# New written order for the first two batches, idle products with a bank of their own, first k and scores in halves

## The chip, the core and the metric

The kernel runs on one core of a Trainium2 chip. The metric is the device time of one execution in microseconds (us), from all inputs in device memory to all outputs in device memory. The engines are named as the profile names them: PE multiplies matrices (PEld is its loading of weights), DVE, ACT and POOL work elementwise, SP issues the DMA transfers.

## The reference

Two layers of attention over 32 packed rows per head, then a max-of-three feed-forward layer, all in float32. Batch 8, 8 heads, 576 rows, head size 64; the scale is 1/8.

```python
def sm_attn(qq, kk, vv):
    s = scale * np.matmul(qq, kk.transpose(0, 1, 3, 2))
    s = s - np.max(s, axis=-1, keepdims=True)
    a = np.exp(s)
    a = a / (np.sum(a, axis=-1, keepdims=True) + 1e-09)
    return np.matmul(a, vv)
p_packed = sm_attn(p, k, v)
out = sm_attn(q, p_packed, p_packed)
...
x = out.transpose(0, 2, 1, 3).reshape(B * S, H * D)
h = np.maximum(np.maximum(x @ w1, x @ w2), x @ w3)      # 512 -> 768
return (h @ w_out).astype(np.float32)                   # 768 -> 512
```

## The kernel before

The work goes batch by batch. Each step has a letter and indices, the first index being the batch b in most of them:

- `S` (scores): p times k for all heads, into two tiles `s1_b_r`, one for each r (even and odd heads, which lie on partitions 0 to 63 and 64 to 127 of k). `A` (weigh, for b < 2 with `turn`): maximum on DVE, exponential on ACT, and in the first two batches a transpose on PE into the bank `tp` and a copy to `a1t`. From batch 2 on `X` does that transpose with DVE and 16 small DMAs (`spread`, tile `xt`). `Z` inverts the sums.
- `V` (values): a1t times v; `K` transposes the packed rows `pp` on PE into `pt_sb`; `Q` (queries): pt times q, in two halves `hf` of 288 columns.
- `C` j c converts one third of the weights of block j: the weights arrive as 64-bit words (load `w` j c, tile `wi`), and ACT (two instructions, L188 and L193), DVE (a shift, L202) and POOL (an add, L206) turn them into `w_sb`. `P` b j (project): pt times w_sb gives the layer-one weights folded with the packed rows, split into `ph` and `pl`.
- `B` b r hf (attend): the softmax of the second attention over 32 packed rows. DVE transposes, takes the maximum, subtracts, ACT exponentiates, DVE sums, inverts, multiplies and transposes back (`et`), and the result is split into `a2h` and `a2l`. Each letter in the text stands for one step of such a generator.
- `N` b j (layer_in): 36 products of 288 columns for each block j of hidden units, six for each of six tiles `mi`. `E` takes the maximum of three, `H` prepares operands, `W` prepares the output weights (loads `w6c`, array `wo`), `O` is the output layer (126 products), `F` sums and stores.

The order of all this is written out by hand as text. `START` holds the words for batches 0 and 1 and the first steps of batch 2, `LOOP` is run for each batch from 2 on. `run` goes through the words; every word issues the next step of its generator, so that the text sets the order of instructions on every engine's queue (loads are words too: they set the order on SP's queue). A suffix v, g or a puts an elementwise instruction on DVE, POOL or ACT instead of its default. Each engine works through its queue in order; it waits where an operand, a buffer or a PSUM bank is not there yet.

SBUF tiles come from pools with few buffers: six for incoming weights (`xs`), eight for k, v, q, a1t and others (`b`). PSUM has two double banks (`ps_big`) and four single ones (`ps_moe`), from which the `mi`, `mo`, first `tp` and first `pw` tiles are taken.

A word `I` n sets n idle products: 128-column products of the identity with itself, which nobody reads. The next step that calls `rouse` issues them into the bank that it is about to use, directly ahead of its own products:

Of the kernel before, what the change touches and what calls it, by code (L numbers as in the profile page):

```python
# [10 lines left out]
F32 = mybir.dt.float32  # L11
# [25 lines left out]
NX, NB, NY = 6, 8, 21  # L37
# [8 lines left out]


START = """
k00 k01 w02 I10 S0 A00 A00 k10 w00 C00 k11 Z00 w22 A00 w01 A01 A01 v01 Z01 C00 C02 C00 C01 v00 I4 S1 A10 A10
q000 C00 A11 I7 A01 A01v V01 C02 C02 A00v Z10 C01 C01 V01 q010 V00 C02 V00 K0 A11 Z11 C01 C22 C22 C22 K0 I1 Q0  # L50
B000 C22 B000 B000 B000 B010 B010 B000 q011 q001 I8 Q0 B011 B010 B010 w12 B001 B000v B000 B000g C12 I3 P00 P00
k20 B001 k21 B011 v11 B001 w10 B011 B010 B010 B000 B000g P00 P00 B001 B011 C12 C12 S2 B001 B000 B001 v10 B001
w11 B010 A21 B001g q10 q11 A21 I10 N00 A20 A20 B011 B010g B010 C12 B011 B011 B011g A10 A11 A10 A11 w21 C11 C11
V101 B010v C10 C10 B011 P00 B001 B001v w20 V101 B010 N00 E000 K1 w32 C11 K1v C10 N00 Q1 B001v C11 B10 C21 B11
C21 E000 E000 C20 N00 C10 P01 P01 B011g C21 C20 w42 C20 C32 w52 P01 B011 P10 X2 N00 N00 E001 E001 C32 C32 C42
C42 C42 C52 C21 w31 N01 E010v C20 w30 C31 C31 E001 B11 N01 v20 E010 N01 P02 C32 E010 C42 C31 C31 N01 w41 N01
w40 P02 P02 C30 E011 E011 C52 C52 N01 C30 P10 C30 X2 C41 C41 N02 P10 E011 N02 E020 E020 C30 B10 N02 C40 C41
Z21 E020 P03 P03 N02 E021 N02 w50 C50 C52 P03 N02 N03 N03 B10 w51 E021 E021 H01 N03 C50 C50 C40 C40 H00v B10
C41 B10 B10 B10 B11v N03 E031v C51 C51 C40 P04 E030v C51 C51 P11 P04 w64 B11 X2 E030 N03 N03 P04 N04 E031 E040
B11 B11 H02v N04 H02 C50 P05 v21 B10g E040 B11 B10 E031 C64 P05 B11g N04 N04 B11 B11 w61 N04 E041v C64 B10g  # L60
P05 B10 N04 C64 B11 w65 C61 w63 V201 E041 C65 C65 E040 E041 H04 H04 N10 E100v C65 N10 C61 C61 E100 Z20 V201
E030 N10 N10 N10 N10 C65 E101v P11 P11 N11 C64 q20 E101 q21 E101 w60 C60 C61 C60 E100 H04v E110v C60 C60 N11
N11 E110 E110 H10 N11 E111 W2v K2 w62 N11 E111 H10g K2 W0v W0 Q2 B20 B21 N11 N05 C63 H01v H00 C62 C62 C62 P13
E050 C63 W0v E111 B20 P12 P12 N05 C62 N05 N05 W0 E050 W2v E050 P12 W0v W2 N05 N05 N12 E051 H00 C63 C63 P13 W1
E120 N12 N12 E051 E051 N12 N12 W0 P14 B21 W2 P13 E120 E120 H03 P15 W2v W2g N12 E121 E121 W0v H01 W1 W1 W1 H02
N13 E121 N13 E130v E130 N13 N13 P14 N13 W1v W1 O0 P14 F0 E130 B20 O0 E131v N13 E131 H03v N14 N14 W1v H03v E131
W1v P15 B21 N14 E140v E140 W1g W1 W2v B21 B21 E140 F0 N14 O0 E141v P15 F0 O0 N14 N14 H05 H05v B20 H05v E141
H03 F0 H01 N15 O0 H12 N15 B20 H05 H13 E150v H01 W0 W2 O0 E141 F0 k30 F0 H03 H01v H14 H05 N15 N15 E151 E150
H03v N15 H05v E150 N15 O0 O0 H12 W0g E151 E151 H15 H13 H12v F0 O0 W2 H14 H13v W0v k31 F0 F0 O0 O0 O0 F0 F0 W2
O0 F0 F0 F0 H10v H14v H11 O0 O1 F1 O1 O1 F1 F1 B20v H15v F0 H15 B21 H11v H11v H13v H13 F0 H13v P20 H11 H11 P20  # L70
P20 H15 P22 P21 B21 P20 P20 O1 F1 H11v H15v O1 O1 H15v F1 F1 O1 B20 B20g O1 O1 F1 O1 F1 F1 B21g B21 B21 O1 F1
F1 O1 P22 P22 B21 P21 O1 F1 B20 P21 F1 B20 O1 F1 F1 B20v F1
"""


# [13 lines left out]
def fused_kernel(ctx: ExitStack, tc: tile.TileContext, kp, qt, va, vb, wi, wo, out):  # L89
# [46 lines left out]
    idle = [0]  # L136

    def rouse(ps):

        k = ps.shape[-1] // P  # L140
        for i in range(0, idle[0], k):
            n = min(idle[0] - i, k)
            nc.tensor.matmul(  # L143
                out=ps[:, 0:n * P], lhsT=ident, rhs=ident.unsqueeze(1).to_broadcast([P, n, P]),
                start=True, stop=True,
            )
# [6 lines left out]
        nc.sync.dma_start(out=t, in_=wi[j, c] if j < NJ else wo[c])  # L153
        staged[j, c] = t

    def load_k(b, g):
        u = b * G + g
        kt = pool.tile([P, 2 * S + 2 * 64], F32, name=f"kt{u}", tag="b", bufs=NB)
        nc.sync.dma_start(out=kt, in_=kp[u])
        loaded["k", b, g] = kt  # L160

    def load_v(b, g):
        u = b * G + g
# [76 lines left out]
    QUADS = [(g, pr) for g in range(G) for pr in range(2)]  # L240
    s1, a1, z1, a1t, av, pp, s2, a2 = {}, {}, {}, {}, {}, {}, {}, {}

    def scores(b):

        kt = [loaded.pop(("k", b, g)) for g in range(G)]
        s1[b] = [ps_big.tile([P, 2, 512], F32, name=f"s1_{b}_{r}", tag="big") for r in range(R)]
        rouse(s1[b][0][:, 0])
        for hf in range(2):
            for n, (g, pr) in enumerate(QUADS):
                for r in range(R):  # L250
                    o = slice(64 * r, 64 * r + 64)
                    w = 2 * S + 64 * pr + 32 * r
                    nc.tensor.matmul(  # L253
                        out=s1[b][r][32 * n:32 * n + 32, hf, 0:HS],
                        lhsT=kt[g][o, w:w + NP],
                        rhs=kt[g][o, pr * S + hf * HS:pr * S + (hf + 1) * HS],
                        start=True, stop=True,
                    )
        yield 0

    def weigh(b, r):

# [342 lines left out]
    def weigh_and_turn(b, r):  # L605
# [4 lines left out]

    stages = {
        "S": scores, "A": weigh_and_turn, "Z": invert, "X": spread, "V": lambda b, *rs: values(b, rs), "K": packed, "Q": queries,
        "B": attend, "C": convert, "P": project, "N": layer_in, "E": maximum, "H": halves,
        "O": layer_out, "F": finish, "W": weights,
    }
    loads = {"k": load_k, "v": load_v, "q": load_q, "w": load_w}
    begun = {}

    def run(words, base):

        for word in words.split():
# [66 lines left out]
```

## Time and profile before

| | us |
|---|---|
| median of 3 runs | 472.49 (471.71 to 473.06) |
| the profiled execution, its time | 472.98 |
| its span, first to last instruction | 471.2 |
| PE busy in it | 457.2 |
| DVE, POOL, ACT busy | 343.6, 218.6, 168.4 |
| scores of batch 3 (first instruction of the first LOOP) | at 147.75 |
| scores of batch 4 (first instruction of the second LOOP) | at 202.00 |

Lists of instructions are read as: start in us, duration in us, engine, line, operation, tiles written and read, shapes, how many were merged into one row, and in brackets how long the engine had been idle and what it waited for. A float32 product appears as two matmul records. Rows with a colon between two times are windows of the span: length, then for each engine its busy time and the number of instructions, then the granted clock of TensorE as a share of full speed (PEclk), the busy share of the DMA engines and GB/s. Rows of the chain that ended last have a start, a duration and the line. Groups have a count, the busy time in all and the mean in ns of one.

### The profile page before, as it was taken

How to read it: one execution, taken by the hardware profiler on the slowest of the kernel's cores; microseconds unless marked ns; L12 is line 12 of the kernel's file. 1: busy time of each engine (PE TensorE's matmuls, PEld its weight loads, DVE VectorE, ACT ScalarE, POOL GpSimd, SP SyncE). 2: the span in 40 equal slices, each digit the busy share in tenths (PEclk: the TensorE clock that was granted, in tenths of full speed). 3: DMA queues.
4: the chain of work that ended last, by engine and by line, in shares of the span. 5: the costliest groups of instructions: out<-in, count | busy, mean ns of one | idle time of the engine just before them, and what ended most of it. 6: DMA issues, size and time to landing. Idle time of an engine off the chain costs nothing.

```text
span 471.2 us, 11512 instructions
## 1 busy us (share of the span) xinstructions
PE 457.2 (97%) x4710; PEld 404.1 (86%) x4710; DVE 343.6 (73%) x722; ACT 168.4 (36%) x325; POOL 218.6 (46%) x193
## 2 busy tenths in 40 slices
PE   7799999999999999999999999999999999999996
PEld 2447887899989898989989898998989898998996
DVE  1669986987888678786777678776787667875652
ACT  3458855634233226122350225212260223402330
POOL 0467784776544055612564037421556036531642
PEclk9889999999999999999999999999999999999999
DMA  8998856002213640082303730064300820020002
GB/s 332 373 379 285 293 159 245 1 1 86 86 65 119 199 127 1 25 282 51 111 1 101 229 105 35 26 204 118 120 1 34 280 41 3 26 75 1 1 4 98
DMA packets 36580, 55.66 MB, mean 118 GB/s; under 512 B 17328, under 2 KB 27568, under 8 KB 36528
## 3 DMA queue, kind: packets, MB, share of 16 engines
q1 hardware_dynamic: 36528, 54.93, 35.4%
q8 instruction: 37, 0.61, 0.5%
q14 instruction: 15, 0.12, 0.1%
HBM read 41.94 MB, written 9.44 MB: 109 GB/s over the span
## 4 chain that ended last, share of the span: by engine, by line
PE 87%; DMA 6%; DVE 3%; ACT 1%; issue 1%; POOL 1%; SPq 1%; DVEq 0%; ACTq 0%; POOLq 0%
PE mi L475 45%; PE mo L544 29%; PE pw L439 7%; DMA wi<-in_wi 3%; DMA v<-in_va 2%; PE av L337 2%; DMA wi<-in_wo 2%; PE s L366 2%; PE s L253 1%; PE s L143 1%; DVE e L389 1%; DVE w_sb L202 1%; DVE r L489 0%; DVE xt L218 0%; PE tp L296 0%
## 5 line engine op out<-in xcount | busy, mean ns | idle before, releaser
L475 PE MATMUL mi<-a2h,ph 128*128 128x288 f32 x576 | 174.0, 302 | 0.6 <-ACT r L129 0.5
L475 PE MATMUL mi<-a2h,pl 128*128 128x288 f32 x576 | 170.0, 295 | 0.2 <-DVE pl L452 0.2
L475 PE MATMUL mi<-a2l,ph 128*128 128x288 f32 x576 | 169.8, 295 | 0.0
L475 PEld LDWEIGHTS mi<-a2h,ph 128*128 128x128 f32 x576 | 108.1, 188 | 15.6 <-issue 9.9
L475 PEld LDWEIGHTS mi<-a2h,pl 128*128 128x128 f32 x576 | 108.1, 188 | 0.7 <-DVE pl L452 0.7
L489 DVE TENSOR_TENSOR r<-mi,r 128x288 f32<-128x288 f32 x192 | 84.2, 449 | 33.3 <-PE mi L475 29.8
L475 PEld LDWEIGHTS mi<-a2l,ph 128*128 128x128 f32 x576 | 108.1, 188 | 0.0
L129 ACT COPY r<-mi 128x288 f32<-128x288 f32 x54 | 20.9, 398 | 120.3 <-PE mi L475 117.2
L452 DVE SCALAR_TENSOR_TENSOR pl<-pw,ph 128x768 fp32r<-128x768 f32 (+1 forms) x61 | 46.6, 772 | 3.2 <-ACT ph L450 2.6
L450 ACT ACTIVATE ph<-pw 128x768 fp32r<-128x768 f32 (+1 forms) x61 | 39.8, 674 | 15.2 <-PE pw L439 14.7
L513 POOL TENSOR_TENSOR r<-r 128x576 f32<-128x576 f32 (+1 forms) x29 | 35.2, 1225 | 20.5 <-issue 9.0
L544 PE MATMUL mo<-ych,xh 128*128 128x288 f32 x144 | 42.5, 295 | 0.0
L544 PE MATMUL mo<-ycl,xh 128*128 128x288 f32 x144 | 42.5, 295 | 0.0
L544 PE MATMUL mo<-ych,xl 128*128 128x288 f32 x144 | 42.4, 295 | 0.0
L134 POOL TENSOR_TENSOR yal<-r,yah 128x576 fp32r<-128x576 f32 x14 | 20.2, 1443 | 47.1 <-ACT yah L129 39.3
L439 PE MATMUL pw<-w_sb,pt 64*32 64x384 f32 x768 | 36.1, 487 | 0.8 <-POOL w_sb L206 0.4
L271 ACT ACTIVATE a<-s,nm 128x576 f32<-128x576 f32 x16 | 11.8, 740 | 65.9 <-DVE nm L267 65.9
L206 POOL TENSOR_TENSOR w_sb<-w_sb,wi 128x512 int32<-128x512 int32 x18 | 23.7, 1326 | 23.2 <-DVE w_sb L202 16.3
L131 DVE COPY r<-mi 128x288 f32<-128x288 f32 x42 | 18.9, 453 | 18.4 <-PE mi L475 18.3
L131 POOL CAST yah<-r 128x576 fp32r<-128x576 f32 x7 | 4.7, 674 | 56.4 <-DVE r L513 56.4
L544 PE MATMUL mo<-yah,xh 128*128 128x288 f32 x96 | 28.9, 301 | 0.0
L544 PE MATMUL mo<-ybl,xh 128*128 128x288 f32 x96 | 28.3, 295 | 0.0
(121 smaller groups left out, 871.6 us busy)
## 6 DMA issues: line engine op xcount, KB each, us to landing
kt<-in_kp SPq DMA_DIRECT2D x16, 640.0 KB, 4.0
wi<-in_wi SPq DMA_DIRECT2D x18, 512.0 KB, 7.6
v<-in_va SPq DMA_DIRECT2D x16, 512.0 KB, 5.7
q<-in_qt SPq DMA_DIRECT2D x14, 576.0 KB, 7.0
wi<-in_wo SPq DMA_DIRECT2D x6, 512.0 KB, 6.1
out_t<-r SPq DMA_DIRECT2D x8, 288.0 KB, 2.4
out_t<-t SPq DMA_DIRECT2D x8, 288.0 KB, 2.3
out_t<-s SPq DMA_DIRECT2D x8, 288.0 KB, 2.7
```

Source lines behind the costliest of these rows:

```text
L129: e.copy(out=out, in_=src)
L131: e.tensor_copy(out=out, in_=src)
L134: on(default).tensor_tensor(out=lo, in0=src, in1=hi.bitcast(F32), op=ALU.subtract)
L206: nc.gpsimd.tensor_tensor(out=dst.bitcast(I32), in0=dst.bitcast(I32), in1=up, op=ALU.add)
L271: nc.scalar.activation(out=a.rearrange("p (a b) -> p a b", a=2), in_=s[:, :, 0:HS], func=AF.Exp, bias=nm, scale=SCALE, accum_out=z,)
L439: nc.tensor.matmul(out=ps[r][NP * n:NP * n + NP, 0:NW * P], lhsT=pt_sb[b % 2][o, NP * n:NP * n + NP], rhs=w_sb[o, j, n * NW * P:(n + 1) * ...
L450: nc.scalar.activation(out=hi[:, r], in_=x, func=AF.Copy, scale=2.0 ** -WS)
L452: nc.vector.scalar_tensor_tensor(out=lo[:, r], in0=x, scalar=2.0 ** -WS, in1=hi[:, r].bitcast(F32), op0=ALU.mult, op1=ALU.subtract,)
L475: nc.tensor.matmul(out=sums[b, j, hf, x][:, 0:HS], lhsT=w[:, r, x * P:(x + 1) * P], rhs=a[:, c], start=(r == 0 and n == 0), stop=(r == R - ...
L489: nc.vector.tensor_tensor(out=h, in0=sums[b, j, hf, i][:, 0:HS], in1=h, op=ALU.max)
L513: less = lambda out, x, y: on("g").tensor_tensor(out=out, in0=x, in1=y, op=ALU.subtract)
L544: nc.tensor.matmul(out=ps[:, 0:HS], lhsT=w[:, x, m * P:(m + 1) * P], rhs=h[:, z], start=(p == 0 and i == 0), stop=(p == NQ - 1 and i == 2),)
```

## The change

Three things change.

1. `START` is written anew: nearly every word stands elsewhere. Batch 0 now goes first: k, q and v of batch 0 and the weights of blocks 0 and 1 are loaded ahead of k, v and q of batch 1. `LOOP` stays as it is, and `START` ends with the same steps done.
2. A new word `J` n issues n idle products at its own place in the order, into a single bank from `ps_moe` taken for them. `I` stays for the first ten.
3. k of batch 0 is loaded by halves of 64 partitions (`k` b g r), and `S0` has two steps, one for each r.

Numbers of lines: what stood at L253, L296, L337, L352, L366, L439 and L475 stands two lines further down in the changed file, the conversion (L188 to L206) one line.

```diff
 START = """
-k00 k01 w02 I10 S0 A00 A00 k10 w00 C00 k11 Z00 w22 A00 w01 A01 A01 v01 Z01 C00 C02 C00 C01 v00 I4 S1 A10 A10
-q000 C00 A11 I7 A01 A01v V01 C02 C02 A00v Z10 C01 C01 V01 q010 V00 C02 V00 K0 A11 Z11 C01 C22 C22 C22 K0 I1 Q0
...
+k000 k010 I10 S0 k011 A00 A00 J9 A00 q00 A00 w00 k001 J3 S0 A01 A01 v00 J9 A01 v01 Z01 C00 C00 Z00 w02 C02
+A01v V00 C00 V00 q01 V01 V01 J2 K0 C00 w01 w10 K0 C02 C02 J1 Q0 B010 C02 B010 B010v C01 C01 w11 B010 C10 C01
...
-    def load_k(b, g):
+    def load_k(b, g, r=None):
         u = b * G + g
-        kt = pool.tile([P, 2 * S + 2 * 64], F32, name=f"kt{u}", tag="b", bufs=NB)
-        nc.sync.dma_start(out=kt, in_=kp[u])
-        loaded["k", b, g] = kt
+        if ("k", b, g) not in loaded:
+            loaded["k", b, g] = pool.tile([P, 2 * S + 2 * 64], F32, name=f"kt{u}", tag="b", bufs=NB)
+        o = slice(0, P) if r is None else slice(64 * r, 64 * r + 64)
+        nc.sync.dma_start(out=loaded["k", b, g][o], in_=kp[u][o])
...
     def scores(b):
 
-        kt = [loaded.pop(("k", b, g)) for g in range(G)]
+        kt = [loaded["k", b, g] for g in range(G)]
         s1[b] = [ps_big.tile([P, 2, 512], F32, name=f"s1_{b}_{r}", tag="big") for r in range(R)]
         rouse(s1[b][0][:, 0])
-        for hf in range(2):
-            for n, (g, pr) in enumerate(QUADS):
-                for r in range(R):
...
-        yield 0
+        for rs in [(0,), (1,)] if b == 0 else [(0, 1)]:
+            for hf in range(2):
+                for n, (g, pr) in enumerate(QUADS):
+                    for r in rs:
...
+            yield 0
...
-        for word in words.split():
+        for at, word in enumerate(words.split()):
...
+            if kind == "J":
+                idle[0] = int(name[1:])
+                rouse(ps_moe.tile([P, 512], F32, name=f"idle{at}", tag="moe"))
+                continue
```

What the new text does to the queues is shown at three places. First, SP's queue at the start of the program (`kt0` and `kt1` are k of batch 0, `kt2` and `kt3` of batch 1, `v0`, `v1`, `q0`, `q1` batch 0, `wi0_2` the third third of the weights of block 0). Before:

```order
L159 DMA kt0_79<-in_kp 128x1280
L159 DMA kt1_81<-in_kp 128x1280
L153 DMA wi0_2_83<-in_wi 128x512
L159 DMA kt2_113<-in_kp 128x1280
L153 DMA wi0_0_115<-in_wi 128x512
L159 DMA kt3_118<-in_kp 128x1280
L153 DMA wi2_2_123<-in_wi 128x512
L153 DMA wi0_1_132<-in_wi 128x512
L165 DMA v1_141<-in_va 128x1024
L166 DMA v1_141<-in_vb 64x256
L165 DMA v0_151<-in_va 128x1024
```

The same place after the change:

```order
L161 DMA kt0_79<-in_kp 64x1280
L161 DMA kt1_81<-in_kp 64x1280 x2
L175 DMA q0_115<-in_qt 128x1152
L153 DMA wi0_0_120<-in_wi 128x512
L161 DMA kt0_79<-in_kp 64x1280
L166 DMA v0_140<-in_va 128x1024
L167 DMA v0_140<-in_vb 64x256
L166 DMA v1_154<-in_va 128x1024
L167 DMA v1_154<-in_vb 64x256
L153 DMA wi0_2_165<-in_wi 128x512
L175 DMA q1_194<-in_qt 128x1152
```

The v tiles of batch 0 moved ahead of most weights, and k of batch 1 to 17th and 19th place behind seven more weight loads.

Second, PE's queue between the packed rows of batch 0 (`av0` and `pa0_1`) and its first projection `pw0_0` (`s2_0_0` and `s2_0_1` are the two halves of the queries). Before:

```order
L352 MATMUL av0_199<-ident_67,pp0_230 128x128
L143 MATMUL s2_0_0_268<-ident_67 128x128
L366 MATMUL s2_0_0_268<-q0_180,pt0_73 32x288 x4
L366 MATMUL s2_0_0_268<-q1_232,pt0_73 32x288 x4
L143 MATMUL s2_0_1_293<-ident_67 128x512 x2
L366 MATMUL s2_0_1_293<-q0_180,pt0_73 32x288 x4
L366 MATMUL s2_0_1_293<-q1_232,pt0_73 32x288 x4
L143 MATMUL pw0_0_0_314<-ident_67 128x384
L439 MATMUL pw0_0_0_314<-w_sb_72,pt0_73 32x384
```

After:

```order
L354 MATMUL pa0_1_148<-ident_67,pp0_192 128x128
L143 MATMUL idle42_228<-ident_67 128x128
L368 MATMUL s2_0_0_230<-q0_115,pt0_73 32x288 x4
L368 MATMUL s2_0_0_230<-q1_194,pt0_73 32x288 x4
L368 MATMUL s2_0_1_253<-q0_115,pt0_73 32x288 x4
L368 MATMUL s2_0_1_253<-q1_194,pt0_73 32x288 x4
L143 MATMUL idle75_288<-ident_67 128x512 x2
L143 MATMUL idle75_288<-ident_67 128x384
L441 MATMUL pw0_0_0_292<-w_sb_72,pt0_73 32x384
```

The two halves of the queries now follow one another, and eleven idle products stand behind them (21 more stand between `pw0_0` and `pw0_1`, and `pw0_1` stands ahead of the first `mi`).

Third, SP's queue around the sixteen small transfers of `X2` (`xt2`), the output weights (`wi6_c`) and q of batch 2. Before:

```order
L153 DMA wi6_4_860<-in_wo 128x512
L319 DMA xt2_863<-x2_596 32x5x64 x8
L319 DMA xt2_863<-x2_596 32x4x64 x8
L165 DMA v5_929<-in_va 128x1024
L166 DMA v5_929<-in_vb 64x256
L153 DMA wi6_1_961<-in_wo 128x512
L153 DMA wi6_5_988<-in_wo 128x512
L153 DMA wi6_3_991<-in_wo 128x512
L174 DMA q4_1112<-in_qt 128x1152
L174 DMA q5_1115<-in_qt 128x1152
L153 DMA wi6_0_1118<-in_wo 128x512
L153 DMA wi6_2_1159<-in_wo 128x512
```

After:

```order
L166 DMA v4_926<-in_va 128x1024
L167 DMA v4_926<-in_vb 64x256
L153 DMA wi6_1_962<-in_wo 128x512
L153 DMA wi6_0_993<-in_wo 128x512
L321 DMA xt2_1022<-x2_823 32x5x64 x8
L321 DMA xt2_1022<-x2_823 32x4x64 x8
L153 DMA wi6_4_1108<-in_wo 128x512
L153 DMA wi6_5_1124<-in_wo 128x512
L175 DMA q5_1135<-in_qt 128x1152
L175 DMA q4_1163<-in_qt 128x1152
L153 DMA wi6_2_1190<-in_wo 128x512
L153 DMA wi6_3_1216<-in_wo 128x512
```

Two output-weight loads and v of batch 2 moved ahead of the sixteen transfers; two other output-weight loads stayed last.

More of the change, by code (lines that the diff above doesn't have):

```diff
@@ L48 @@
 START = """
-k00 k01 w02 I10 S0 A00 A00 k10 w00 C00 k11 Z00 w22 A00 w01 A01 A01 v01 Z01 C00 C02 C00 C01 v00 I4 S1 A10 A10
-q000 C00 A11 I7 A01 A01v V01 C02 C02 A00v Z10 C01 C01 V01 q010 V00 C02 V00 K0 A11 Z11 C01 C22 C22 C22 K0 I1 Q0
-B000 C22 B000 B000 B000 B010 B010 B000 q011 q001 I8 Q0 B011 B010 B010 w12 B001 B000v B000 B000g C12 I3 P00 P00
-k20 B001 k21 B011 v11 B001 w10 B011 B010 B010 B000 B000g P00 P00 B001 B011 C12 C12 S2 B001 B000 B001 v10 B001
-w11 B010 A21 B001g q10 q11 A21 I10 N00 A20 A20 B011 B010g B010 C12 B011 B011 B011g A10 A11 A10 A11 w21 C11 C11
@@ L54 @@
[L54 to L72, printed above, removed]
+k000 k010 I10 S0 k011 A00 A00 J9 A00 q00 A00 w00 k001 J3 S0 A01 A01 v00 J9 A01 v01 Z01 C00 C00 Z00 w02 C02
@@ new lines @@
+A01v V00 C00 V00 q01 V01 V01 J2 K0 C00 w01 w10 K0 C02 C02 J1 Q0 B010 C02 B010 B010v C01 C01 w11 B010 C10 C01
+C01 Q0 w12 C10 B001 B000 B001 B000 B001v B000v C10 C10 C11 C11 C11 B000 C11 B000 B010 w20 C12 J11 P00 P00 w22
+B011 P00 B000 B000 C12 B011 B001 P00 C12 C12 J21 P01 k10 B000 B000 B010 B001 C20 w32 k11 w21 B000 B000 B010
+B001 N00 B010 B010 B010g C22 C22 P01 P00 B010 N00 B001 B011v B001g v11 S1 v10 B011 P01 C32 C32 N01 N01 N01 C20
+B011 w30 E000v C22 B011v B001 E010 A11 A11 A10 A10 E010 Z11 B001v C21 C20 C21 C22 N00 B001v B011 E000 A10 A11
@@ new lines @@
+q10 A10v E000 q11 A11 N00 B011g B011 B011 V101 C20 C30 C30 w31 B011 Z10 E010 N01 V101 C21 C21 K1 C30 N00 w52
+C31 K1v C32 C32 Q1 N00 E011 E001 B10 C31 w41 P02 P02 B11 C52 P10 P10 B10 w40 B11 k20 C40 C41 C31 P02 N01 E011
+C30 N01 C31 P03 B10 P03 E001 E001 C41 N02 N02 E020 N02 C52 N02 E011 k21 N02 H00 w42 B10 B11 P10 E021 P03 S2
+C40 E020 C40 N03 N03 N03 v21 C41 C41 C42 E020 B11 C42 B10 E021 C52 E030 C42 A20 A20 A21 A21 w50 C50 w51 B11
+B11 B10 X2 X2 C50 C50 C51 N02 C52 N03 C40 C42 P04 C51 C50 B10 E030 E030 P11 B11 N03 B11g N03 C51 B10g P04 C51
@@ new lines @@
+P04 E031 N04 N04 N04 P05 E031 B11 v20 B11 E040v E040 B10 H01 H01v N04 N04 N04 E021 w61 C61 E031 P05 E041 P05
+N05 N05 N05 E040 w60 C60 B10g B10 B11 H00 N10 C61 E041 P11 Z20 E050 H00v X2 C60 C60 E041 C61 E050 P11 V201 Z21
+V201 N11 N11 K2 w64 N10 C61 E110v E110 E050 H01 H01 w65 C65 C65 N11 q21 N11 N10 K2 E100v N10 H04v H04 q20 Q2
+N11 w62 N10 E111 E110 C60 W0v N10 W0v W0v W0 w63 W0 H02v H02 E101 C65 P13 H04v B20 E100 B21 E101 C65 W0 E111
+E100 P12 N11 C62 C62 C63 C63 P13 C62 P12 W0v H03 C64 N05 C63 E101 N05 N05 C63 E051v P12 E051 C64 C64 P13 N12
@@ new lines @@
+N12 E111 C62 H01 H03v W1v W1v W1v N13 H02v N13 N13 E120 E130 P14 W1 P15 P15 E130 N12 C64 W2 W2 E051 N12 E121
+W1v N13 E131 E130 P14 W2v W2g W0 P15 E120 E120 N13 E131 W2v N12 E121 N12 E121 W0g W0 H05g P14 W2g O0 O0 W1 W2v
+B21 W2 N14 N14 W1v B20 N13 E131 H03 H05 F0 E140 O0 E140 F0 N14 E140 H12v H03v O0 k31 F0 N14 H05 N14 N15 N15
+N15 B20v H11 H05v E141 N14 E141 H01v W2 H10v W1v E150 B21v E150 E141 H03 F0 H03v W1g N15 N15 E151 E151 O0 H10g
+H10v H05 O0 H05v O0 B21 E150 W2 F0 F0 H13 H13 N15 E151 H14v O0 F0 F0 O0 B20 F0 O0 O0 B20 W1v H12 O0 F0 H12 H14
@@ L73 @@
+H11 F0 F0 F0 O0 H13v O0 H13v H13 H14 P20 P20 P22 F0 F0 H15 P21 H11v B21 F0 H15v P22 O1 O1 F1 k30 P20 O1 O1 O1
+O1 P21 H15v H15v H11v H15 H13v P22 H11g H11v B20v H15v O1 P20 F1 O1 B20 B20g O1 O1 O1 F1 O1 F1 B21 B21 F1 F1
+B21g F1 O1 F1 P20 B20 B20v O1 F1 F1 F1 B21 F1 F1 P21 F1 F1 B21 B21 B20v F1
 """
@@ L243, in scores @@
     def scores(b):
-        kt = [loaded.pop(("k", b, g)) for g in range(G)]
+        kt = [loaded["k", b, g] for g in range(G)]
         s1[b] = [ps_big.tile([P, 2, 512], F32, name=f"s1_{b}_{r}", tag="big") for r in range(R)]
         rouse(s1[b][0][:, 0])
-        for hf in range(2):
-            for n, (g, pr) in enumerate(QUADS):
-                for r in range(R):
[L251 to L258, printed above, removed]
-        yield 0
+        for rs in [(0,), (1,)] if b == 0 else [(0, 1)]:
+            for hf in range(2):
+                for n, (g, pr) in enumerate(QUADS):
+                    for r in rs:
+                        o = slice(64 * r, 64 * r + 64)
+                        w = 2 * S + 64 * pr + 32 * r
+                        nc.tensor.matmul(
+                            out=s1[b][r][32 * n:32 * n + 32, hf, 0:HS],
+                            lhsT=kt[g][o, w:w + NP],
+                            rhs=kt[g][o, pr * S + hf * HS:pr * S + (hf + 1) * HS],
+                            start=True, stop=True,
+                        )
+            yield 0
     def weigh(b, r):
```

## The prediction

> **What bounds the kernel now.** I read the page first, then windows of the span, then PE's list for the first 32 us, then the chain of waits.
>
> ```profile
> span 471.2 us, 11512 instructions
> PE   7799999999999999999999999999999999999996
> PEclk9889999999999999999999999999999999999999
> GB/s 332 373 379 285 293 159 245 1 1 86 86 65 119 199 127 1 25 282 51 111 1 101 229 105 35 26 204 118 120 1 34 280 41 3 26 75 1 1 4 98
> ```
>
> PE is full in 37 of 40 slices, so time can only come from the start, where it is not full or its clock is low, or from the last slice, which the change leaves alone.
>
> ```profile
> 7.50:9.50 2.00, 0.04 (x1) 0.04 (x1) 0.97 (x3) 0.83 (x2) 0.00 (x0) 1.00 1.01 417
> 14.50:19.60 5.10, 2.55 (x83) 1.79 (x85) 3.69 (x11) 4.37 (x9) 2.44 (x2) 0.97 1.06 323
> 19.60:26.10 6.50, 6.06 (x38) 2.15 (x42) 3.09 (x9) 1.66 (x4) 2.76 (x4) 0.50 1.04 409
> 31.40:61.30 29.90, 28.21 (x354) 22.02 (x352) 27.32 (x64) 24.37 (x48) 21.23 (x20) 1.00 0.81 285
> 61.30:100.90 39.60, 38.07 (x424) 33.24 (x417) 33.95 (x68) 21.46 (x37) 29.90 (x26) 1.00 0.35 117
> 100.90:147.80 46.90, 46.90 (x387) 44.80 (x393) 38.56 (x70) 17.14 (x31) 27.32 (x24) 1.00 0.19 60
> ```
>
> The columns are PE, PEld, DVE, ACT, POOL. From 19.6 to 26.1 the granted clock is 0.50. From 31.4 on PE loses 1.7 us, then 1.5, then nothing, and DVE is as good as full from 31.4 to 61.3. What PE does before that:
>
> ```profile
> 5.81 1.67 PE L253 MATMUL s<-kt 64*32 64x288 f32 x32
> 9.46 0.66 PE L296 MATMUL tp<-ident,a 128*128 128x128 f32 x4 [1.98 <-ACT a L271]
> 18.01 0.90 PE L337 MATMUL av<-v,a1t 128*32 128x64 f32 x40 [2.55 <-DMA v<-in_va]
> 18.84 1.09 PE L337 MATMUL pa<-v,a1t 128*32 128x64 f32 x40
> 20.37 0.48 PE L352 MATMUL av<-ident,pp 128*128 128x128 f32 x1 [0.44 <-DVE z L282]
> 21.20 1.21 PE L366 MATMUL s<-q,pt 64*32 64x288 f32 x16
> 22.34 3.78 PE L143 MATMUL s<-ident 128*128 128x512 f32 x4
> 26.05 0.72 PE L366 MATMUL s<-q,pt 64*32 64x288 f32 x16
> 29.32 2.42 PE L143 MATMUL mi<-ident 128*128 128x512 f32 x6
> 31.38 0.48 PE L475 MATMUL mi<-a2h,ph 128*128 128x288 f32 x1
> ```
>
> PE waits 2.55 us for v, the clock drops a microsecond later, and eight idle products at half clock (3.78 us) stand ahead of the second half of the queries, which starts at 26.05 instead of 22.4. The first useful large product starts at 31.38.
>
> ```profile
> 7.58 10.29 DMA v<-in_va
> 59.90 1.45 PE pw L439 x32
> 61.35 0.72 PE mi L475 x4
> 147.75 1.13 PE s L253 x32
> ```
>
> The chain runs through that v load. Two marks serve below. At 61.35 PE has just done the pair P04 and P11, with 132 products of `mi` behind it; in the new order the same pair stands behind exactly the same 132 products and the same other steps. At 147.75 the first LOOP starts, with equal work done in both orders; from there nothing changes.
>
> **The change, part by part.** The sum is made on the profiled execution (472.98, 0.49 above the median of the runs).
>
> *Loads.* By the GB/s row 3.9 MB have landed after one slice of 11.8 us, 8.3 after two, 12.8 after three. In the new order v of batch 0 is complete after 3.6 MB (about 11 us; before 17.87), all q of batch 0 after 4.7 (14 us), block 0 of the weights after 5.2 (15 us), block 1 after 6.8 (20 us), block 2 after 10.2 (29 us). The halved k adds two issues to SP's queue and the undivided q takes two away: nothing, since the ninth load waits for a free slot behind eight anyway.
>
> *Scores in halves.* Before, 16 products (32 records) of both r take 1.67 us; at full clock 1.13 (the row at 147.75). A half has 16 records. Lower bound 0.57 us; upper bound 1.13, since r = 0 and r = 1 lie on different halves of the partitions and would run side by side. I take 1.13. The Trainium skill, "TensorE: Matmul & The Clock Gate", Part 3 on packing small matmuls, speaks against the halves: products run concurrently when they lie in different row groups, and a half uses one group of 64 rows only. By that rule the two halves cost 2.26 together, by the record count 1.13; on the chain to the first product that is 1.1 us. No row of this trace has such a half.
>
> *Chain to the queries.* S0 for r = 0 ends at 5.8 + 1.1 = 6.9; maximum and exponential take until the transpose what they took before (7.48 to 9.46, 1.98), so the transpose is at 8.9. J9 fills that gap: idle products cost 2.02 us per ten at full clock (29.34 to 31.36), so J9 costs 1.8 and delays nothing. Transpose (0.8), J3 (0.6), second half of the scores (1.1) to 11.5; 1.98 more, covered by the second J9, to 13.5; transpose to 14.3, V00 and V01 with 0.9 each and the copy of a1t between them to 16.3. v is there since 11. From the end of V to the queries it took 19.93 to 21.20, 1.27: queries at 17.6. Since the gaps are filled, the clock should stay whole, and both halves (0.72 each) are done at 19.0, before at 26.8.
>
> *Queries to the first N.* DVE is the long pole. Its queue holds 21 instructions from the first transpose to `et`:
>
> ```profile
> L389 DVE STREAM_TRANSPOSE e<-s 128x288 f32<-128x288 f32 x32 | 13.9, 463 | 4.6 <-PE s L366 4.6
> L393 DVE TENSOR_REDUCE m<-e 128x9 f32<-128x288 f32 x4 | 1.7, 437 | 0.1
> L400 DVE TENSOR_REDUCE z<-e 128x9 f32<-128x288 f32 x4 | 1.8, 446 | 0.4 <-ACT e L397 0.4
> L395 DVE TENSOR_TENSOR e<-e,m 128x576 f32<-128x576 f32 x1 | 0.7, 694 | 0.0
> L452 DVE SCALAR_TENSOR_TENSOR pl<-pw,ph 128x384 fp32r<-128x384 f32 x26 | 13.7, 548 | 2.2 <-ACT ph L450 1.7
> L134 POOL TENSOR_TENSOR a2l<-et,a2h 128x288 fp32r<-128x288 f32 x3 | 2.4, 799 | 0.2
> L202 DVE TENSOR_SCALAR w_sb<-wi x18: 408/424/1442, 12.1 to 61.0; 128x512 uint32<-128x512 uint32 x18
> L206 POOL TENSOR_TENSOR w_sb<-w_sb,wi x18: 1281/1318/1397, 12.7 to 62.8; 128x512 int32<-128x512 int32 x18
> L188 ACT ACTIVATE wi<-wi x24: 647/678/717, 10.4 to 82.5; 128x512 f32<-128x512 f32 x24
> ```
>
> Five transposes (2.3), four maxima (1.75), three subtractions and one multiplication at half of 694 (1.4), four shifts (1.7), two sums (0.9), one `pl` (0.55), one reciprocal (0.2): 8.8 us from 18.3, so `et` at 27.1; the ACT cast (0.4) and `a2l` (0.8) follow to 28.3. The third weight piece of block 1 needs its DVE shift (about 26.1) and then 1.3 on POOL, so P01 ends near 27.8. J11 and J21 (32 idle products, 6.5 us) lie between 19.0 and 26.5 in that gap and are hidden; without that cover they would cost 6.5. First N at 28.0, before 31.38: −3.4. Ends: 26.5 if the halves take 0.57 and DVE's pairs overlap, 30.5 if ACT, which has ten conversion instructions of 0.68 in the same stretch, holds up the exponentials.
>
> *Work that changes sides.* Before, S1 and S2 (1.13 each) were done ahead of the first N, and P01 (0.72) behind it; now the other way round: +1.5 by the mark P04, P11. Between first N and that mark PE lost 3.5 us before (29.97 less 26.5 of work). In the new order I find: 0.9 at the transposes of batch 1 (DVE's maxima), 0.4 at V1, 0.5 at `a2l` of the first N, 0.9 at P03 and 1.1 at P04, whose last weight adds on POOL stand behind DVE shifts that follow B1's transposes and maxima. That is 3.8: no gain, no loss beyond 0.3. Mark at 61.35 − 3.4 + 1.5 + 0.3, about 59.7.
>
> *From the mark to the first LOOP.*
>
> ```profile
> 79.75 0.67 ACT L188 ACTIVATE wi<-wi 128x512 f32<-128x512 f32 x1 [4.74 <-DMA wi<-in_wo]
> 80.00:84.00 4.00, 2.96 (x46) 1.00 0.03 9
> 84.00:88.00 4.00, 3.60 (x48) 1.00 0.01 2
> 155.88 10.83 SPq L319 DMA_DIRECT2D xt<-x  x16
> ```
>
> ACT waits until 79.75 for an output-weight load, the copies of `mi` behind it come late, and PE loses 1.04 and 0.40 us. In the new order the two last loads still land near 80, but ACT's instructions for them stand behind the copies that PE needs until about 86. Between 0 and −1.4; I take −1.2, since they no longer meet. V2 waits for the sixteen transfers of X2: S2's end + 4.2 (maxima, exponentials, DVE transposes) + 10.83 + some 2 to land = 17; PE has 16.1 of work between S2 and V2, and the 1.1 of P04: no wait, without margin.
>
> *The rest.* Buffer and dictionary edits issue nothing. Idle banks are taken while only `tp` and `pw` use those four: nothing.
>
> Sum: −3.4 + 1.5 + 0.3 − 1.2 = −2.8; 472.98 − 2.8 = 470.2, on the median 472.49 − 2.8 = 469.7.
>
> **Rivals.**
>
> *A, the converter is the bound (no change).* DVE was busy 27.32 of 29.90 us from 31.4 to 61.3 and POOL adds cost 1.32 each. If P03 and P04 wait 2 us longer than I find, the start's gain is gone by the mark: 472.5. For it: block 3 and 4 are now due earlier, and DVE holds their shifts behind softmax work. Against it: POOL had 8.7 us free in that window.
>
> *B, V2 waits for the spread (slower).* In the new order S2 stands behind N02, where before it was done at 29. If the second DVE transpose of X2 ends 4.2 us later than S2's end + 4.2, the gain is gone and 1.4 more: 473.9 and up; every further microsecond goes straight into the time, since V2 stands in PE's queue. For it: there is no margin, and DVE's queue is full. Against it: only maxima, a sum and two shifts stand ahead there.
>
> *C, the clock drops anyway.* If the 0.50 comes from the small products of V and Q and not from the gap of 2.55 us, it also meets the new order: 6.5 us at half clock lose 3.3, which makes 473.0. Against it: small products at 5.8 to 15 ran at 1.00, also behind the gap of 1.98 us from 7.5 to 9.5. The Trainium skill, the same page, Part 1 on the clock gate, speaks of an idle window of about 3.4 us before the clock is halved. By that the gap of 2.55 in this trace would be too short to be the cause, which would favour C; the trace has the drop right behind the gap.
>
> *D, a larger gain.* PE's waits behind the first N shrink by 1.5 and the first N comes at 26.5: 466.7.
>
> **How the numbers follow.** About 0.3% (1.4 us) is what a measurement of this kernel can tell from no change. Forecast (1.4 to 4.4 us faster) 0.55; D 0.12; A 0.13; C 0.06; B 0.14. Faster 0.67, same 0.19 (A and C), slower 0.14. Predicted 469.7. The range leaves out the outer part of D and of B: 466.2 (D with the whole 1.4 of the late stall) to 474.0; the forecast alone is 468.1 to 471.1.
>
> **What would show it.** First `mi` product near 28.0 (no later than 29.5); PEclk 1.00 from 6 us on; queries at 17.6 with no idle products between the halves; P04, P11 pair ending near 59.7; no wait of PE for `wo` between 78 and 88; first LOOP's scores near 145. Wrong it would be by a clock of 0.50 after 16 us, by PE waiting more than 2 us at P03 or P04 for POOL, or by V2 waiting for `xt`.

## The result, and the profile after

The changed kernel takes 469.86 us (median of 9 runs, 468.8 to 471.68), the kernel before 472.6 beside it: a ratio of 0.9942 (95% interval 0.9919 to 0.9964). The forecast was 469.7. The total is right; several steps under it are not, and that their errors cancelled is luck. The experiments found a version at 466.7.

Each run reports its mean granted clock. In three of the nine runs it is 0.994 to 0.996 and the time 471.5 to 471.7; in six it is 0.998 to 1.000 and the time 468.8 to 470.2. The profiled execution (471.49, span 469.7) is one of the three. Three executions far above all others are left out of every comparison below (634 us at a clock of 0.657, which is the one with the trace of e1_whole_k, 883 us and 2516 us). The page of the profiled execution:

```profile
span 469.7 us, 11526 instructions
PEclk9899999999999999999999999999999999999999
GB/s 220 372 360 341 397 93 288 3 22 35 36 148 155 165 124 1 27 285 62 96 1 115 219 125 11 27 223 103 118 1 43 278 34 2 27 75 1 1 4 98
```

PEclk was 8 in the second and third slice before; the third is now whole, but the dip in the second is still there, where the forecast said there would be none. The first figure of GB/s is the other surprise: 220, before 332. Windows of 2 us (columns as before: PE, PEld, DVE, ACT, POOL, granted clock, DMA share, GB/s), first of the kernel before, then of the changed one:

```profile
4.00:6.00 2.00, 2.00 (x8) 0.83 (x10) 0.00 (x0) 0.00 (x0) 0.00 (x0) 1.00 1.01 411
6.00:8.00 2.00, 1.48 (x32) 0.44 (x24) 0.47 (x1) 0.00 (x0) 0.00 (x0) 1.00 1.02 422
```

```profile
4.00:6.00 2.00, 2.00 (x6) 0.75 (x6) 0.00 (x0) 0.00 (x0) 0.00 (x0) 1.00 1.00 210
6.00:8.00 2.00, 2.00 (x17) 0.79 (x18) 0.00 (x1) 0.00 (x0) 0.00 (x0) 1.00 0.94 258
14.00:16.00 2.00, 2.00 (x6) 0.84 (x3) 0.91 (x2) 0.50 (x1) 0.00 (x0) 0.50 1.05 327
```

The DMA engines are as busy in both (share about 1.0), yet move half as much from 4 to 6 us (210 against 411 GB/s), while the half loads of k are at the head of the queue. PE's list of the profiled execution, with the products of Q2 and of the first LOOP at its end:

```profile
13.06 1.32 PE L255 MATMUL s<-kt 64*32 64x288 f32 x16 [1.73 <-DMA kt<-in_kp]
14.31 3.71 PE L143 MATMUL idle<-ident 128*128 128x512 f32 x6
18.50 1.83 PE L339 MATMUL pa<-v,a1t 128*32 128x64 f32 x80
21.45 1.21 PE L368 MATMUL s<-q,pt 64*32 64x288 f32 x32
31.98 0.40 PE L477 MATMUL mi<-a2h,ph 128*128 128x288 f32 x1
59.60 1.52 PE L441 MATMUL pw<-w_sb,pt 64*32 64x384 f32 x32
80.58 1.21 PE L368 MATMUL s<-q,pt 64*32 64x288 f32 x32 [1.03 <-DMA q<-in_qt]
146.22 1.20 PE L255 MATMUL s<-kt 64*32 64x288 f32 x32
```

PE waits for the second half of k until 13.06. The clock then falls (0.50 from 14 to 16 us), and the second J9 takes 3.71 where 2.21 is its length at full clock. The first mi product comes at 31.98, later than before (31.38), and the time was won behind it.

The same kernel, profiled once more (e8_changed_again, 469.96, clock 0.999), shows the ordinary case without the dip; it is the one to hold against the forecast:

```profile
5.92 1.70 PE L255 MATMUL s<-kt 64*32 64x288 f32 x16
12.30 1.17 PE L255 MATMUL s<-kt 64*32 64x288 f32 x16 [1.28 <-DMA kt<-in_kp]
13.40 2.21 PE L143 MATMUL idle<-ident 128*128 128x512 f32 x6
16.18 1.84 PE L339 MATMUL pa<-v,a1t 128*32 128x64 f32 x80
19.14 1.20 PE L368 MATMUL s<-q,pt 64*32 64x288 f32 x32
29.76 0.40 PE L477 MATMUL mi<-a2h,ph 128*128 128x288 f32 x1
57.45 1.52 PE L441 MATMUL pw<-w_sb,pt 64*32 64x384 f32 x32
70.35 1.44 PE L339 MATMUL av<-v,xt 128*32 128x64 f32 x74 [0.33 <-DMA xt<-x]
78.97 1.29 PE L368 MATMUL s<-q,pt 64*32 64x288 f32 x32 [1.31 <-DMA q<-in_qt]
144.68 1.20 PE L255 MATMUL s<-kt 64*32 64x288 f32 x32
```

From the first LOOP to the end nothing changed: 471.2 − 147.68 = 323.5 before, 468.2 − 144.68 = 323.5 here.

### The profile page after: what moved, and what is told of

The parts are those of the page before. It is cut to its first block, busy times and chain, and to the rows that moved or that the text cites. A ratio compares the mean times of both kernels' runs of the same rounds, so it can differ in the third digit from the quotient of the medians.

```text
span 469.7 us, 11526 instructions
## 1 busy us (share of the span) xinstructions
PE 460.6 (98%) x4726; PEld 407.0 (87%) x4726; DVE 344.7 (73%) x727; ACT 168.7 (36%) x331; POOL 212.1 (45%) x182
## 4 chain that ended last, share of the span: by engine, by line
PE 83%; DMA 5%; DVE 5%; SPq 3%; issue 1%; POOL 1%; ACT 1%; POOLq 0%; DVEq 0%
PE mi L477 42%; PE mo L546 29%; PE pw L441 6%; SPq L321 2%; DMA kt<-in_kp 2%; PE av L339 2%; PE s L368 2%; DMA wi<-in_wi 2%; PE s L255 1%; DMA q<-in_qt 1%; PE idle L143 1%; POOL w_sb L207 1%; DVE w_sb L203 1%; DVE mx L268 1%; DVE pl L454 0%
## 5 line engine op out<-in xcount | busy, mean ns | idle before, releaser
L129 ACT COPY r<-mi 128x288 f32<-128x288 f32 x61 | 23.7, 400 | 122.4 <-PE mi L477 122.3
L515 POOL TENSOR_TENSOR r<-r 128x576 f32<-128x576 f32 (+1 forms) x23 | 26.9, 1180 | 17.3 <-issue 9.0
L131 DVE COPY r<-mi 128x288 f32<-128x288 f32 x35 | 15.9, 456 | 18.2 <-PE mi L477 18.1
L515 DVE TENSOR_TENSOR r<-r 128x288 f32<-128x288 f32 (+1 forms) x49 | 27.1, 556 | 2.3 <-POOL ybl L134 1.7
```

The lines of the kernel that those rows point to most:

```text
L129: e.copy(out=out, in_=src)
L131: e.tensor_copy(out=out, in_=src)
L515: less = lambda out, x, y: on("g").tensor_tensor(out=out, in0=x, in1=y, op=ALU.subtract)
```

## Experiments

The theory after the result (R): a load that touches only 64 partitions moves at half the rate, and holds up what is queued behind it. The rivals: the place of the last half behind q and w (P), the converter as the bound (C), and that all of the gain is the clock (K). The letter C stands for the converter in this section only; the prediction calls that rival A.

**k loaded whole, scores still in halves (e1_whole_k).**

```diff
-k000 k010 I10 S0 k011 A00 A00 J9 A00 q00 A00 w00 k001 J3 S0
+k00 k01 I10 S0 A00 A00 J9 A00 q00 A00 w00 J3 S0
```

> The changed kernel with both k of batch 0 loaded whole (128 partitions each) as the first two transfers, ahead of q and w; the first scores still in two halves. Theory R (rate): a load that touches only 64 partitions moves at about half the rate, 210 GB/s where the kernel before had 411 from 4 to 6 us, and holds up all loads queued behind it; that made the second half of k land at 13.0. By R the GB/s from 2 to 8 us go back to about 290, 410, 420; both k are there near 5.9; the second half of the scores starts at 10.5 to 11 with no wait of PE for k; no 0.50 of the clock; queries near 18.5; first mi product at 28 to 29.5 instead of 31.98; the pair P04, P11 ends 1.0 to 2.5 earlier than 61.05; time 0.9 to 2.5 us below the changed kernel, 467.4 to 469.0. Rival C (the converter is the bound): the start comes as early, but PE then waits the same 2 to 3 us more at P01 to P04 for weights, the pair ends at 61 and the time stays within 0.5 us of 469.9. Rival P (place in the queue): the half load was late only because q and w stood ahead of it; then the rate from 2 to 8 us is about as low as in the changed kernel, since what sets it would not be the halves.

Measured: 467.93, ratio to before 0.9901 (0.9877 to 0.9926), 1.9 us below the changed kernel, as R said; C, which allowed 0.5, is out. Only its time is used here, so what R said of its single steps is not shown by this run.

**The last half load moved to the front (e1b_half_k_early).**

```diff
-k000 k010 I10 S0 k011 A00 A00 J9 A00 q00 A00 w00 k001 J3 S0
+k000 k010 I10 S0 k011 k001 A00 A00 J9 A00 q00 A00 w00 J3 S0
```

> The changed kernel with its four half loads of k kept, but the last of them moved ahead of q and w. Theory R: four loads of 320 KB at about 210 GB/s take some 6.2 us, so the last half of k is there near 9; PE does not wait for it at 10.5 to 11; q, w and v stay as late as in the changed kernel (the sum of bytes and rates is the same), v complete near 15; low rate from 2 to 8 us and none of the dip to 208 from 10 to 12; first mi product 29 to 30.5; time between e1_whole_k and the changed kernel, 468 to 469.5. Rival P: the rate from 2 to 8 us is 290 to 420 now, because nothing but the place was wrong, and k is complete near 6. Rival C: time within 0.5 us of 469.9 here as well.

Measured: 469.62, ratio 0.9939 (0.9917 to 0.9962). Windows, then PE:

```profile
4.00:6.00 2.00, 2.00 (x6) 0.76 (x6) 0.00 (x0) 0.00 (x0) 0.00 (x0) 1.00 1.00 210
6.00:8.00 2.00, 2.00 (x18) 0.79 (x19) 0.44 (x1) 0.00 (x0) 0.00 (x0) 1.00 1.01 205
10.00:12.00 2.00, 2.00 (x22) 0.76 (x19) 0.00 (x0) 0.74 (x2) 0.00 (x0) 1.00 1.03 412
```

```profile
10.84 1.17 PE L255 MATMUL s<-kt 64*32 64x288 f32 x16
28.82 0.85 PE L441 MATMUL pw<-w_sb,pt 64*32 64x384 f32 x8 [0.39 <-POOL w_sb L207]
29.60 0.40 PE L477 MATMUL mi<-a2h,ph 128*128 128x288 f32 x1
```

PE's wait for k is gone, but the rate is low for as long as half loads run and then doubles: the halves set it, not the place, and P is out. The time I gave was 468 to 469.5, a hair too low, and rival C would have had it (within 0.5 of 469.9); it is e1_whole_k that speaks against C. The first mi product comes only 0.16 earlier than in e8_changed_again. What PE no longer waits for k, it loses at P01, which takes from 27.58 to 29.60 here and 1.0 there: it waits for the weight add on POOL, which ends at 28.76 here and at 28.93 there. ACT, which converts these weights first, waits for their loads 1.47, 0.84 and 1.08 long (14 to 22 us; 0.42 and 0.21 there). So half loads cost twice: by the wait for k, and by the weights that stand behind them in the queue.

**Part three undone (e2_whole_scores).** The line of START as in e1_whole_k without the second S0, and:

```diff
-        for rs in [(0,), (1,)] if b == 0 else [(0, 1)]:
+        for rs in [(0, 1)]:
```

> The third part of the change undone: k loaded whole and the first scores of both halves in one step, as before, all else of the new order kept. Theory R: as e1_whole_k; the scores take 1.67 at 5.8 in one piece, the second transpose can start a microsecond earlier, first mi product within 1 us of e1_whole_k; time within 0.8 us of e1_whole_k, so halving the scores buys nothing without the loads. Rival H: the halves of the scores are worth their order, and this run is over 1 us slower than e1_whole_k. Rival C: 469.4 to 470.4.

Measured: 466.78, ratio 0.9882 (0.9855 to 0.9908); 1.15 below e1_whole_k. That is more than the 0.8 I allowed, and rival H, which had it slower, is out.

```profile
4.00:6.00 2.00, 2.00 (x8) 0.75 (x10) 0.00 (x0) 0.00 (x0) 0.00 (x0) 1.00 1.03 416
5.92 1.66 PE L255 MATMUL s<-kt 64*32 64x288 f32 x32
13.39 1.83 PE L339 MATMUL pa<-v,a1t 128*32 128x64 f32 x80
26.91 0.40 PE L477 MATMUL mi<-a2h,ph 128*128 128x288 f32 x1
54.72 1.52 PE L441 MATMUL pw<-w_sb,pt 64*32 64x384 f32 x32
141.70 1.20 PE L255 MATMUL s<-kt 64*32 64x288 f32 x32
```

The scores of both halves take here (1.66) what the first half alone takes in e8_changed_again (1.70), so the half loads did not even bring the first half sooner. The second half costs 1.10 more (12.30 to 13.40): the halves of the scores cost 1.1, their loads the rest. The first mi product is 2.85 earlier, the pair P04, P11 2.73, the first LOOP 2.98: all of it reaches the end, and the converter keeps pace even then. (The two traces are of different chips; e9_whole_again, this kernel on the chip of e8_changed_again, has the first mi product at 26.68 and the first LOOP at 141.69.)

**Part three alone, in the old order (e4_before_halves).**

```diff
-k00 k01 w02 I10 S0 A00 A00
+k000 k010 k011 k001 w02 I10 S0 S0 A00 A00
```

> The kernel before with part three alone: the four half loads of k in place of two whole ones at the head of the queue, and the first scores as two steps one behind the other; the order of all else is that of before. Theory R: k is complete near 8.8 instead of 5.8, everything queued behind it lands some 3 us later (v of batch 0 near 20.5 instead of 17.87), PE's wait for v grows by as much, and the time is 2 to 4 us above before, 474.5 to 476.6. Rival P (the halves cost nothing by themselves): time within 0.5 us of 472.6, k there near 6. Rival: the clock falls one step earlier in the longer gap, then up to 5 us above.

Measured: 476.05, ratio 1.0059 (1.0029 to 1.009): slower, as R said.

```profile
6.00:8.00 2.00, 1.48 (x16) 0.57 (x16) 0.47 (x1) 0.00 (x0) 0.00 (x0) 1.00 1.01 203
9.39 2.11 PE L255 MATMUL s<-kt 64*32 64x288 f32 x16 [1.91 <-DMA kt<-in_kp]
20.82 0.90 PE L339 MATMUL av<-v,a1t 128*32 128x64 f32 x40 [1.80 <-ACT a L273]
```

The second half of the scores begins at 9.39, where before both halves began at 5.81 and were done at 7.48. The products of v come 2.8 later than at 18.01, behind ACT's exponential and not, as I expected, behind v. The wait of 1.91 was enough for the clock to fall to 0.50 (from 10 to 16 us).

**The idle steps taken out of e2_whole_scores (e3_no_idle_steps, e10_no_idle_again).** All J words are dropped from START.

> e2_whole_scores without its seven idle steps (J9, J3, J9, J2, J1, J11, J21), all else the same; PE then stands idle some 2 us before each of the first two transposes, 2.5 us before P00 and 4.5 us before P01. Theory K (the idle products are worth their clock): the granted clock falls to 0.50 in at least one of the longer gaps; if it falls before P01, P01 and the first 3 us of mi products run at half speed and the time is 1.5 to 3 us above e2_whole_scores, 468.3 to 469.8; in the runs where it falls the mean granted clock is 0.993 to 0.997. Rival N (they are worth nothing): clock 1.00 at the first mi product, which comes at 26.9 or earlier, and the time stays within 0.5 us of 466.8. Rival W (idle steps delay work): first mi product 0.3 to 1 us earlier than 26.91 and the time below 466.4.

Measured: 468.33, ratio 0.9910 (0.9889 to 0.9931), with a clock of 0.982 to 0.989, further down than the 0.993 to 0.997 I gave. It ran on another chip than e2_whole_scores, so both were run again side by side, with the changed kernel:

> e3_no_idle_steps again, on one chip with e9_whole_again, which alone it is compared with. Theory K: 1 to 2 us above e9_whole_again, since first mi product came at 28.61 and not 26.91 with the clock at 0.50 in three stretches. Rival N: within 0.5 us of it.

> e2_whole_scores again, beside the changed kernel and the kernel without idle steps on one chip. Theory R: 2 to 3.5 us below e8_changed_again, clock 0.998 to 1.000 in every run. In e5_late_q2 the pair P04, P11 and the product behind it waited 1.0 us in all (at 54.65 and 58.33) where e2_whole_scores did not; if that belongs to the chip, it shows here too and the time is 467.5 to 468; if it belongs to the moved Q2, the time is 466.5 to 467.

> The changed kernel itself, on one chip with the next three. In its profiled execution the clock fell to 0.50 from 14 to 17 us behind a wait of 1.73 us for the second half of k. Theory R: the wait is in every run, since the loads are the same; whether the clock falls varies from run to run: granted clock 0.998 to 1.000 where it does not and 469 to 470.3, 0.994 to 0.996 where it does and 471.3 to 471.8. Rival: the wait is an accident of that one run, then the first mi product is at 28 to 29 and the time 468.

Measured on one chip: before 472.99, without idle steps 468.42 (ratio 0.9925, 0.9897 to 0.9953), with them 466.71 (0.9883, 0.9858 to 0.9907), the changed kernel 469.81 (0.9943, 0.9923 to 0.9963). So the idle steps are worth 1.7 us, and the granted clock of each run says the same: 0.981 to 0.989 without them, 0.998 to 1.000 with them. The dip of the changed kernel, which I expected in some of its runs, was in none of these eleven (clock 0.998 to 1.000), though the wait for k was there in the one with a trace, 1.28 long. The trace without idle steps, and behind it the same place in e9_whole_again:

```profile
12.00:14.00 2.00, 2.00 (x48) 1.28 (x46) 1.48 (x6) 0.85 (x3) 0.14 (x1) 0.54 1.00 363
11.71 0.74 PE L298 MATMUL tp<-ident,a 128*128 128x128 f32 x4 [1.45 <-ACT a L273]
20.66 0.87 PE L441 MATMUL pw<-w_sb,pt 64*32 64x384 f32 x12 [2.30 <-POOL w_sb L207]
23.23 2.74 PE L441 MATMUL pw<-w_sb,pt 64*32 64x384 f32 x8 [1.71 <-POOL w_sb L207]
26.27 1.51 PE L441 MATMUL pw<-w_sb,pt 64*32 64x384 f32 x8 [0.30 <-POOL w_sb L207]
27.71 0.61 PE L477 MATMUL mi<-a2h,ph 128*128 128x288 f32 x1
```

```profile
25.77 0.98 PE L441 MATMUL pw<-w_sb,pt 64*32 64x384 f32 x16
26.68 0.40 PE L477 MATMUL mi<-a2h,ph 128*128 128x288 f32 x1
```

The idle products hold up no real work: in e9_whole_again P01 begins at 25.77, as they end, and the last weight add that it needs ends on POOL at 25.85. Without them PE waits for the weights of P00 and P01 in the same places, the clock falls to 0.50 from 24 to 28 us, and the first mi product comes 1.0 later.

**Only the gap filled, in the old order (e7_before_filled_gap, e11_before_short_fill).** J12, then J5, ahead of the first V01 of before, with the changed kernel's code for J:

```diff
-q000 C00 A11 I7 A01 A01v V01 C02
+q000 C00 A11 I7 A01 A01v J12 V01 C02
```

> The kernel before with one thing added: an idle step of 12 products (2.4 us) behind the second transpose, where PE waits 2.55 us for v; order, loads and scores as before. Theory K (what the changed kernel gained is the clock): the 0.50 from 19.6 to 26.1 is gone, the eight idle products between the halves of the queries take 1.6 instead of 3.78, the second half starts at 23 to 24 instead of 26.05, first mi product near 29, and the time is 470.0 to 471.0, so the changed kernel's gain of 2.7 would nearly all be had without the new order. Theory O (the order of loads and steps): the second half of the queries then waits for its q load or the first mi product for DVE and POOL; first mi product 30.5 or later, time 471.8 to 472.5, and the new order's gain is its own.

Measured: 472.11, ratio 0.9988 (0.9975 to 1.0001). The time is in the range of theory O, but not for its reason: the idle step was too long for its gap: it could begin only at 16.74, since its bank came free late, and v's products were put off to 19.51. With J5:

> e7_before_filled_gap with 5 idle products in place of 12. There the idle step began only at 16.74, since its bank came free late, ended at 19.5, and so put off the products of v by 1.5 us. With 5 (1.0 us) they start near 18.0 to 18.3 as in the kernel before, with the clock at 1.00 in runs where it stays whole. Theory K (the clock): second half of the queries near 23.7, first mi product near 29.2, time 470.8 to 471.3. Theory O (order of loads and steps): the first mi product comes no earlier than 30 because weights or DVE end last, time 471.6 to 472.4.

Measured: 471.41, ratio 0.9977 (0.9957 to 0.9997), between the two theories' ranges.

```profile
16.62 1.35 PE L143 MATMUL idle<-ident 128*128 128x512 f32 x4 [0.68 <-DVE a1t L131]
23.88 0.71 PE L366 MATMUL s<-q,pt 64*32 64x288 f32 x16
27.61 1.17 PE L253 MATMUL s<-kt 64*32 64x288 f32 x24 [0.87 <-DMA kt<-in_kp]
30.78 0.48 PE L475 MATMUL mi<-a2h,ph 128*128 128x288 f32 x1
```

The clock is 0.995 to 1.000 in its runs (0.988 to 0.996 in most runs of before), the second half of the queries came at 23.88 instead of 26.05, and then a new wait stood there: S1 for its k. So in the old order a whole clock is worth about 1.1 (ratio 0.9977 of 472.99; by the interval 0.1 to 2.0). Most of the gain belongs to the order: with whole loads, and with a lower clock than before had (0.981 to 0.989), the new order is 4.6 faster in e10_no_idle_again.

**Q2 written later (e5_late_q2).**

```diff
-H04v H04 q20 Q2
-N11 w62 N10 E111
+H04v H04 q20
+N11 w62 N10 Q2 E111
```

> e2_whole_scores with the step Q2 written two N steps (12 products, 1.6 us) later. PE waits there 1.18 us for the queries' load at 74.51. If that wait is on the path: gone, first LOOP 1.0 to 1.2 us earlier than 141.70 and the time 465.6 to 466.0. Rival: the work behind Q2 (its transposes on DVE, the spread, P12) comes later by as much and PE waits elsewhere: time within 0.4 us of 466.8.

Measured: 468.23, ratio 0.9905 (0.9886 to 0.9924), against 466.71 to 466.78 for the kernel it is made from: no gain, rather a loss. The wait moved:

```profile
76.00 0.40 PE L477 MATMUL mi<-a2h,ph 128*128 128x288 f32 x1 [0.30 <-ACT r L129]
77.81 0.40 PE L477 MATMUL mi<-a2h,ph 128*128 128x288 f32 x1 [0.74 <-ACT r L129]
81.03 0.40 PE L477 MATMUL mi<-a2h,ph 128*128 128x288 f32 x1 [1.01 <-DVE r L491]
```

The two N steps ahead of Q2 and the one behind it then wait for banks that ACT and DVE have not yet emptied, 2.05 in all, where e9_whole_again waits 1.50 for q. The wait for q had covered these. (This execution also lost 1.0 at 54.65 and 58.33; e9_whole_again, on the same chip, did not, and e3_no_idle_steps did, on that chip too, so neither the chip nor the moved Q2 decides it. What does stays open.)

## Why the prediction was right in sum and wrong in parts

Measured against e8_changed_again, whose clock stays whole.

- **Loads: failed.** The step that called the halved k "nothing" looked at the issues on SP's queue and took the rate from the row of before. While only loads of 64 partitions run, the rate is 203 to 220 GB/s (from 4 to 6 us 210 and 215 in the two traces of the changed kernel; from 4 to 8 us 205 to 210 in e1b_half_k_early and 203 to 220 in e4_before_halves), where whole ones had 411 and 422 before. The Trainium skill, "SBUF — State Buffer", section "Door 1: The DMA port swizzle", states just this: partitions 0 to 63 reach 8 of the 16 ports, and a 1 MiB transfer to them was measured there at 196 GB/s. The traces here agree with it; the prediction did not use the page. Undoing part three gives 3.1 us (469.81 to 466.71): some 1.9 from the loads and 1.2 from the scores (469.86, 467.93, 466.78).
- **Scores in halves: the cost of a half was right.** Taken 1.13, measured 1.10. Part 3 of "TensorE: Matmul & The Clock Gate" in the Trainium skill, cited against the halves, is borne out: a half alone takes 1.10, and both side by side take 1.13 (the row at 147.75). The first half I put at 1.1 after 5.8; it took 1.70 at that place, as the whole does there (1.66), and was 0.65 late.
- **Chain to the queries: mis-sized by 1.5.** Forecast 17.6, measured 19.14: 0.65 by the first half, 1.28 by the wait of the second half for k (it began at 12.30, with 10.4 in the forecast), and 0.4 won back, most of it at V. From there to the first mi product the working holds, 10.6 measured against 10.4. First mi product 29.76, forecast 28.0; in the execution with the dip 31.98. The −3.4 was −1.6.
- **Clock: right as a rule, not in every run.** The gap of 2.55 was the cause of the 0.50, since filling it alone (e11_before_short_fill) keeps the clock whole; the prediction's rival C is out. But the change made a gap of its own, 1.28 and 1.73 long in the two traces, and in 3 of 20 runs (3 of 9, 0 of 11) the mean clock was lower, at some 1.7 us each. One of the three has a trace, and there the fall stands right behind that gap.
- **Work changing sides and stalls: the other large error.** From the first mi product to the end of the pair it took 29.1 (29.76 to 58.90), with 26.5 + 1.5 = 28.0 of work: stalls of 1.1 by the forecast's way of counting, where I found 3.8 and before had 3.5. (By PE's rows it stood idle 0.13 there, before 1.69.) The waits at P03 and P04 for weight adds were not there, and the prediction's rival A is out: not even with the first mi product 3 us earlier did they come (e2_whole_scores: 26.91 to 56.17, 29.3). The +0.3 was −2.3. So the pair ended at 58.9, with 59.7 in the forecast.
- **Late stall: failed.** Forecast −1.2, since PE's two waits behind ACT would be gone. From the pair to the first LOOP it took 86.40 before (61.28 to 147.68 in PE's list) and 85.78 after, −0.6. But PE waits as long as it did. Before (the second wait is put down to DVE):

```profile
81.47 1.21 PE L366 MATMUL s<-q,pt 64*32 64x288 f32 x32 [1.04 <-ACT pt L129]
84.86 1.52 PE L439 MATMUL pw<-w_sb,pt 64*32 64x384 f32 x32 [0.40 <-DVE e L389]
```

  After, it waits 0.33 for `xt` and 1.31 at Q2 for q, which is issued only when V2 has freed its buffer. In all PE stood idle 1.53 in this stretch before and 1.89 after; its equal number of products was busy for 84.87 and 83.89. Why they took less is not shown. ACT's work for `wo` still stood ahead of copies that PE needs: e5_late_q2 brings these waits to light.
- **Rival B** (V2 behind the spread) was near: V2 waits 0.33 for `xt`, one of the signs that the forecast named for being wrong. It did not decide.
- **Sums of the rivals.** Two do not come out of their own terms: 2 us more at P03 and P04 make 471.7 for A (473.7 if each is meant) and not 472.5, and the whole 1.4 of the late stall makes 466.5 for D and not 466.2.

Sum as measured: −1.6 + 1.5 − 2.3 − 0.6 = −3.0, and the span of e8_changed_again is 468.2 against 471.2. The forecast's −3.4 + 1.5 + 0.3 − 1.2 = −2.8 came out near it because the start was 1.8 too early, the stalls 2.6 too long and the late gain 0.6 too large. That these cancel is luck: none of the three is the reason for another in the working.

By parts, on one chip, each on top of the one before it: the new order with whole loads and no idle steps −4.6 (472.99 to 468.42), idle steps −1.7, halves of k and scores +3.1.

## What to carry to other kernels

Price a split load by the rate, not by its bytes: halved across partitions it ran here at half the rate, and everything queued behind it paid. Taking away the wait that one sees is then not enough, since the loads behind are late too (e1b_half_k_early). When the parts of a change pull in both directions, a correct total says little; profile where each part ends. Idle products pay where PE waits anyway (1.7 us here), if they are shorter than the wait and their bank is free when it begins.

## What the runs showed of the hardware

- The clock fell behind waits of 1.45 (e10_no_idle_again, after one of 1.98), 1.73 (the changed kernel), 1.91 (e4_before_halves) and 2.55 us (before), and did not fall behind 1.98 in the profiled run of before or 1.28 in e8_changed_again. So the length of one wait does not decide alone. In the changed kernel the mean clock differed between runs of one program. The Trainium skill, "TensorE: Matmul & The Clock Gate", Part 1, describes a window of about 3.4 us that runs freely of the program. The difference between runs would agree with that, but the two traced runs differ in the length of the wait too (1.73 and 1.28), so no run here shows it; the section's reading that a gap must be longer than that window to bring the clock down does not agree with these waits.
- Half-partition loads keep the DMA share at 1.0 while they move half as much (1.00 at 210 GB/s against 1.01 at 411, from 4 to 6 us), so the busy share of the DMA engines does not show that a queue is slow. The GB/s does.
